# Attention and a gated block on one core: idle products on PE in the first stage, a shorter distance table, the remainder of v on halves of PE's columns, and a planner with other costs

## The chip, the cores and the metric

The program runs on one core of one Trainium2 chip. The metric is the time of one execution on the device in microseconds (us); the time of the kernel before is the median of three runs. Engines are named as the profile names them: PE does the matrix products, DVE is the vector engine, ACT the scalar engine, POOL the general one, and SP's queue issues the transfers.

## The reference

Eight batches, eight heads, 576 positions, 64 numbers a head. Attention looks back over a window of 128 positions with a slope a head (the distance table is `-8*slope*distance`, with a huge number where the mask is zero). Its result is the input of a block with a gate: a product with w_in, halves u and v, a normalisation of v, a mixing of v along the positions, a product with w_out.

```python
scores = scale * np.matmul(q, k.transpose(0, 1, 3, 2))
scores = np.where(mask, scores + bias[None], -1000000000.0)   # 0 <= rel < 128
attn = softmax(scores)                    # sum + 1e-9
x = np.matmul(attn, v)                    # -> [8, 576, 512]
h = np.maximum(x @ w_in, 0.0)             # 512 -> 1024
u, v = h[..., :512], h[..., 512:]
v_n = (v - mean(v)) / np.sqrt(var(v) + 1e-06)
v_s = np.einsum('ts,bsd->btd', w_spatial, v_n) + b_spatial[None, :, None]
out = (u * v_s) @ w_out
```

## The kernel before

Heads are taken in pairs: a batch has four pairs (p), and a pair has five tiles (t) of query blocks, the first with one block of 64 rows, the others with two. Float32 accuracy comes from splitting a number into two 16-bit parts, so a product is made of three.

**The first stage** is batch 0 (and pair 0 of batch 1), done without such a split: `raw_tile` and `raw_rest` make the scores as float32 products (L581, L582), take bias, minimum and exponential (DVE L614, ACT L619), turn the result around on PE (L651, L653), copy it (L325) and multiply with the values (L671). Beside it the weights are prepared: w_in comes as 64-bit numbers in four chunks a half (transfer L364, tile `vn`), which `words` turns into float32 (ACT L341, DVE L345 to L357) and `magnitudes` into absolute values (ACT L373, tile `ab`); the mixing weights (transfers L441 to L449, tile `gw`) get absolute values in ACT L460, L464, L465. `column_scale` sums such absolute values over the partitions on PE, with `ones` as the stationary operand (L384). `largest` finds the scale of a batch's values (ACT L554, DVE L502 and L503, PE L505, DVE L507, then POOL L524, L525 and DVE L527).

**Later batches** make the probabilities in two 16-bit parts (L720, L754, L759), a transposing transfer turns them around (L765), and `attention` multiplies them with the values on two halves of PE's columns at a time (L798: 72 products, in 36 pairs that write to partitions 0 to 63 and 64 to 127). Each pair of heads leaves a tile `xt` with the high part of x, a piece of R = 64 columns, and the low part: `tail` copies the last 64 low columns behind the high ones (L532, recorded in the helper's line L325), so that `v_rem` can use high and low part of the last 64 positions as one stationary operand of 128 columns.

**The gated block** (`gated`) has units of 12 to 14 products that fill the PE: `v_unit` (L864, 128x512 each, 12 a unit, four units a batch), `v_rem` for the last 64 positions (L886, 8 products of 128x512: a stationary operand for each of the four chunks, times two parts of w_in; upper and lower half of the result are added afterwards), `u_unit` (L916), `sp_unit` (L937) and `o_unit` (L965).

**The order** on every engine is made when the program is built: `Plan` collects each piece of work with its engine, a weight in ns, a due time and what it reads and writes; `order` is a list scheduler that models the engines (and two levels of PE's clock), and `emit` runs it forward and backward 20 times and takes the best. An engine then executes its work strictly in that order. A row of 64-row products and a row of 128-row products use PE's array in different shapes (64*64, 128*64, 128*128 in the rows); the planner has the constant SWITCH for that.

## Time and profile before

| what | value |
|---|---|
| median of 3 runs | 577.02 us (574.56 to 577.95) |
| the profiled execution's own time | 573.75 us |
| its span, first to last instruction | 572.0 us |
| PE busy | 542.9 us, 95% of the span |
| DVE busy | 466.8 us, 82% |
| ACT busy | 418.0 us, 73% |
| POOL busy | 65.7 us, 11% |

The shares are means over stages with different limits. The profiled execution lies 0.81 us below the fastest of the three timed runs, and 1.75 us of its time lie outside the span.

### The profile page before, as it was taken

The page shows a single profiled execution, that of the slowest core. Times are in us where ns is not written, and L with a number is a line of the kernel's source. Part 1 is how long each engine was busy: PE and PEld are TensorE (multiplying, and loading weights), DVE is VectorE, ACT ScalarE, POOL GpSimd, SP SyncE. Part 2 cuts the span into 40 slices and gives each one's busy share as a digit, 9 for nine tenths or more (in the row PEclk, how much of TensorE's full clock was granted, in tenths as well). Part 3 has the DMA queues.
Part 4 walks back from the last instruction along what each step waited for, and adds up shares of the span by engine and source line. Part 5 has one row for each costly group of instructions (what it writes and reads, how often), then busy time and mean ns, then how long its engine had stood idle before and what let it go on. Part 6 is the DMA issues. An engine that isn't in the chain of part 4 may idle for free.

```text
span 572.0 us, 16995 instructions
## 1 busy us (share of the span) xinstructions
PE 542.9 (95%) x6472; PEld 386.2 (68%) x6475; DVE 466.8 (82%) x1794; ACT 418.0 (73%) x1389; POOL 65.7 (11%) x124
## 2 busy tenths in 40 slices
PE   3399998899999999999999999999999999999997
PEld 2155646677668866787578757887587758785775
DVE  4779999999998589987899689888998788764541
ACT  5979999999996298767877587679996657543202
POOL 2001122000124002010131001200202011000000
PEclk9999999999999999999999999999999999999999
DMA  8961321698998275794468787769677650460002
GB/s 276 324 260 48 117 93 43 151 185 175 241 212 161 58 182 104 143 227 132 114 139 218 164 157 120 161 162 223 140 127 127 136 115 1 84 138 32 1 11 72
DMA packets 149845, 79.74 MB, mean 139 GB/s; under 512 B 129666, under 2 KB 139906, under 8 KB 149764
## 3 DMA queue, kind: packets, MB, share of 16 engines
q1 hardware_dynamic: 149764, 78.67, 58.8%
q8 instruction: 50, 0.82, 0.6%
q14 instruction: 31, 0.25, 0.1%
HBM read 37.13 MB, written 9.44 MB: 81 GB/s over the span
## 4 chain that ended last, share of the span: by engine, by line
PE 72%; DVE 1%; ACT 1%; issue 0%; ACTq 0%
PE m L937 17%; PE m L965 15%; PE m L916 14%; PE m L864 11%; PE x L798 6%; PE s L582 6%; PE m L886 2%; ACT prob L720 0%; ACT pq L754 0%; DVE st L825 0%; DVE vt L838 0%; ACT vt L329 0%; DVE vn L875 0%; ACT o L972 0%; DVE vn L325 0%
## 5 line engine op out<-in xcount | busy, mean ns | idle before, releaser
L720 ACT ACTIVATE prob<-prob,stat 64x64 f32<-64x64 f32 (+1 forms) x270 | 113.4, 424 | 15.1 <-DVE stat L714 15.0
L937 PE MATMUL m<-wsp,vn 128*128 128x288 f16 x768 | 113.0, 286 | 0.1
L916 PE MATMUL m<-xt,win 128*128 128x288 f16 x768 | 100.6, 286 | 1.2 <-DVE win L404 0.6
L965 PE MATMUL m<-gs,wout 128*128 128x288 f16 x768 | 100.2, 286 | 0.0
L754 ACT ACTIVATE pq<-prob,stat 64x64 f16<-64x64 f32 x270 | 93.8, 423 | 3.5 <-ACT prob L720 1.0
L759 DVE SCALAR_TENSOR_TENSOR pq<-prob,stat,pq 64x64 f16<-64x64 f32 x270 | 90.4, 378 | 2.0 <-ACT pq L754 1.8
L916 PEld LDWEIGHTS <-win 128*128 128x128 f16 x768 | 73.8, 98 | 22.5 <-issue 3.0
L937 PEld LDWEIGHTS <-vn 128*128 128x128 f16 x768 | 73.9, 98 | 21.2 <-issue 2.7
L965 PEld LDWEIGHTS <-wout 128*128 128x128 f16 x768 | 73.7, 98 | 20.8 <-issue 2.2
L864 PE MATMUL m<-win,xt 128*128 128x512 f16 x384 | 86.4, 379 | 0.9 <-ACT pq L325 0.9
L714 DVE CUSTOM_DVE_ANT_0 prob<-s,tab 64x64 f32<-64x64 f32 (+1 forms) x270 | 73.3, 317 | 7.2 <-PE s L582 7.1
L582 PE MATMUL s<-qkraw 64*64 64x192 f32 (+2 forms) x1116 | 60.0, 325 | 7.5 <-DMA qkraw<-in_qk_dram 6.1
L864 PEld LDWEIGHTS <-xt 128*128 128x128 f16 x384 | 36.9, 98 | 44.4 <-issue 1.9
L834 POOL TENSOR_TENSOR st<-st,nhalf 128x1 f32<-128x1 f32 (+1 forms) x40 | 29.2, 732 | 302.2 <-DVE st L830 289.3
L972 ACT ACTIVATE o<-m,am 128x288 f32<-128x288 f32 x49 | 24.2, 497 | 46.1 <-PE m L965 36.1
L945 DVE TENSOR_TENSOR u<-m,u 128x288 f32<-128x288 f32 x64 | 28.8, 450 | 35.1 <-PE m L937 35.0
L582 PEld LDWEIGHTS s<-qkraw 64*64 64x64 f32 x1116 | 41.4, 137 | 22.0 <-issue 10.8
L720 ACT ACTIVATION_READ_ACCUMULATOR prob<-prob,stat 64x1 f32 (+1 forms) x270 | 51.6, 191 | 0.0
L329 ACT ACTIVATE u<-m 128x288 f32<-128x288 f32 x57 | 23.0, 403 | 38.2 <-PE m L916 37.9
L798 PEld LDWEIGHTS <-vh 128*64 128x64 f16 x1296 | 39.9, 112 | 7.6 <-issue 7.3
L798 PE MATMUL x<-pt,vh 128*64 128x64 f16 (+1 forms) x1296 | 43.1, 205 | 0.1
L798 PE MATMUL x<-pt,vl 128*64 128x64 f16 (+1 forms) x648 | 40.1, 204 | 0.0
(154 smaller groups left out, 786.3 us busy)
## 6 DMA issues: line engine op xcount, KB each, us to landing
qkraw<-in_qk_dram SPq DMA_DIRECT2D x28, 576.0 KB, 4.2
vb<-in_v_dram SPq DMA_DIRECT2D x32, 320.0 KB, 5.0
out_dram<-o SPq DMA_DIRECT2D x64, 144.0 KB, 2.0
vn<-in_w_in_dram SPq DMA_DIRECT2D x8, 512.0 KB, 7.1
pt<-in_w_out_dram SPq DMA_DIRECT2D x4, 512.0 KB, 5.8
gw<-in_w_spT_dram SPq DMA_DIRECT2D x4, 288.0 KB, 8.1
qkraw<-in_qk_dram SPq DMA_DIRECT2D x3, 320.0 KB, 5.6
pt<-pq SPq DMA_TRANSPOSE x54, 5.3
```

What stands on the lines that cost most here:

```text
L582: nc.tensor.matmul(sc[j]()[out, at:at + k1 - k0], raw()[rows, 0, i * D:(i + 1) * D], raw()[rows, 1, k0:k1], start=True, stop=True, skip_gr ...
L714: nc.vector.tensor_tensor_reduce(pt(), sc[t][j]()[:m, SOFF[t]:SOFF[t] + n], tabs[h]()[:m, W - n:], -0.125, 3e38, ALU.add, ALU.min, st()[:m ...
L720: nc.scalar.activation(pt(), pt(), AF.Exp, bias=st()[:m, NM, j, t:t + 1], scale=-1.0, accum_out=st()[:m, SM, j, t:t + 1])
L754: nc.scalar.activation(pq[j]()[:m, 0, qs], prob[2 * (p % 2) + j]()[:m, cs], AF.Copy, scale=st()[:m, RC, j, t:t + 1])
L759: nc.vector.scalar_tensor_tensor(pq[j]()[:m, 1, qs], prob[2 * (p % 2) + j]()[:m, cs], st()[:m, RC, j, t:t + 1], pq[j]()[:m, 0, qs], ALU.mu ...
L798: nc.tensor.matmul(xp()[j * D:(j + 1) * D, x0:x0 + n * D], l()[:, kt, j * D:(j + 1) * D], rhs, start=(i > 4, j) not in seen, stop=False, s ...
L834: nc.gpsimd.tensor_tensor(st()[:m, 11:12], st()[:m, 10:11], nhalf()[:m], ALU.pow)
L864: nc.tensor.matmul(pt(), xt[c]()[:, X0[a] + t * P:X0[a] + (t + 1) * P], win()[:, c, w, DH:DF], start=(n == 0), stop=(n == 3 * NC_ - 1))
L916: nc.tensor.matmul(pt()[:, :HS], win()[:, c, w, d * P:(d + 1) * P], xt[c]()[:, X0[a] + hf * HS:X0[a] + (hf + 1) * HS], start=(n == 0), sto ...
L937: nc.tensor.matmul(pt()[:, :HS], l, r, start=(n == 0), stop=(n == len(ops) - 1))
L945: nc.vector.tensor_tensor(u(), pt()[:, :HS], u(), ALU.mult)
L965: nc.tensor.matmul(pt()[:, :HS], wout()[:, d, w, e * P:(e + 1) * P], gs[d]()[:, a, :], start=(n == 0), stop=(n == 3 * ND - 1))
```

## The change

Four things change. (1) `warm` puts 120 products of 128x192, in 24 pieces of five, into the plan; they multiply `ones` with the distance tables into a bank of the PSUM tag `x` that nobody reads. In the plan 16 pieces wait for ACT's second sum over the values, 8 for the absolute values of w_in; these waits exist in the plan alone, the instructions themselves wait for nothing but `ones`, the tables and the bank. (2) The distance table is made for 64 rows on POOL and copied to the other 64 by DVE. (3) `tail` is gone, `xt` is 64 columns shorter, and `v_rem` makes 12 products of 64x512, in six pairs, one of each pair on either half of PE's columns: high part times both parts of w_in, low part times the high part of w_in (the product of the two low parts is no longer made). (4) The planner no longer adds SWITCH to every piece; each piece has a mode for its first and last product (F: whole array, S: 64*64, X: 128*64), and a change of mode costs TURN = 95 ns. Weights of some pieces are set anew, and transfers issued between 1200 and 8000 ns land 1300 ns later in the plan.

```diff
+    TURN, NEAR = 95, 0
...
                     if e == "SP":
...
-                        end = dma + self.LAG[e]
+                        end = dma + self.LAG[e] + 1300 * (1200 <= now < 8000)
                     else:
+                        if e == "PE":
+                            weight += self.TURN * (modes[n][head] != mode)
+                            mode = modes[n][rear]
...
-            for a in (0, D):
-                rel = relf()[a:a + D]
...
-        plan.add("POOL", 2450, 0, f, (), [(relf, 0)])
+            rel = relf()[:D]
...
+        plan.add("POOL", 1250, 0, f, (), [(relf, 0)])
+        plan.add("DVE", 250, 800, lambda: nc.vector.tensor_copy(relf()[D:], relf()[:D]), [(relf, 0)], [(relf, 1)])
...
-    def tail(xt, due):
-
-        copy(R, lambda: (xt()[:, S:S + R], xt()[:, 2 * S:2 * S + R]), due, xcols(xt, 1, (NQ - 1) * P, S), [(xt, 2)], fast=True)
...
-        plan.add("PE", SWITCH // 2 + scored_ns(t), due, lambda: scored(sc, t, 0, raw), seen_by(raw, t) + [(ones, 0), (masked, 0)], [(sc[j], t) for j in range(2)])
+        plan.add("PE", scored_ns(t), due, lambda: scored(sc, t, 0, raw), seen_by(raw, t) + [(ones, 0), (masked, 0)], [(sc[j], t) for j in range(2)], "SS")
...
-                n = 0
-                for c in range(NC_):
-                    for w in range(2):
-                        nc.tensor.matmul(pt(), xt[c]()[:, (NQ - 1) * P:S + R], win()[:, c, w, DH:DF],
-                                         start=(n == 0), stop=(n == 2 * NC_ - 1))
-                        n += 1
+                sides = [[(0, w, c) for c in range(NC_)] + [(1, 0, c) for c in range(w, NC_, 2)] for w in range(2)]
+                for n, pair in enumerate(zip(*sides)):
+                    for side, (a, w, c) in enumerate(pair):
+                        nc.tensor.matmul(pt()[side * R:(side + 1) * R], xt[c]()[:, X0[a] + (NQ - 1) * P:X0[a] + S], win()[:, c, w, DH:DF],
+                                         start=(n == 0), stop=(n == 3 * NC_ // 2 - 1), skip_group_check=True)
...
+    idle = plan.buf(ps, "x", 2, [P, 512], F32)
+
+    def warm(n, k, due, after):
+
+        def f():
+            for i in range(n):
+                nc.tensor.matmul(idle()[:, :W], ones(), tabs[(k + i) % H](), start=True, stop=True)
+        plan.add("PE", n * pe(W, gap=2.5), due, f, after + [(ones, 0)] + [(tabs[(k + i) % H], 0) for i in range(n)], [(idle, k)])
...
+    for k in range(16):
+        warm(5, k, -20000 + 500 * k, [(am0, ("sum", 1))])
...
+    for k in range(16, 24):
+        warm(5, k, -20000 + 500 * k, [(wv[k % 4][1], 0)])
```

Line numbers of the changed kernel are other ones: its L588 and L589 are L581 and L582 here, L1020 is the idle product, L516 is L505, L395 is L384, L868 is L864, L890 is L886, L548 is L541, L558 is L551, L375 is L364, L452 to L460 are L441 to L449.

The first place is PE early in the first stage, after the second tile's scores of pair 0. Before, the scores of pair 1 and pair 2 follow one another (`s` is the scores' bank, `masked` fills what lies outside the window), then L505:

```order
L582 MATMUL s_69<-qkraw 64x192
L581 LDWEIGHTS ones
L581 MATMUL s_66<-masked,ones 64x64
L582 MATMUL s_66<-qkraw 64x128
L581 LDWEIGHTS ones
L581 MATMUL s_67<-masked,ones 64x64
L582 MATMUL s_67<-qkraw 64x128
L582 MATMUL s_66<-qkraw 64x192
L582 MATMUL s_67<-qkraw 64x192
L505 LDWEIGHTS ones
L505 MATMUL m<-wide,ones 128x128
```

In the changed kernel the idle products stand behind pair 1:

```order
L589 MATMUL s_69<-qkraw 64x192
L1020 LDWEIGHTS ones
L1020 MATMUL x<-tab_76,ones 128x192
L1020 LDWEIGHTS ones
L1020 MATMUL x<-tab_77,ones 128x192
```

30 of them, then L516, then 60 more, which end ahead of pair 2:

```order
L516 LDWEIGHTS ones
L516 MATMUL m<-wide,ones 128x128
L1020 LDWEIGHTS ones
L1020 MATMUL x<-tab_82,ones 128x192
...
L1020 MATMUL x<-tab_76,ones 128x192
L588 LDWEIGHTS ones
L588 MATMUL s_66<-masked,ones 64x64
L589 MATMUL s_66<-qkraw 64x128
```

The second tile's scores of pairs 2 and 3 moved behind 90 idle products; the last 30 stand between pair 3 and the twelve products of the mixing weights (L395, before L384).

The second place is SP's queue from its start (`qkraw` and `pt` are queries and keys of the four pairs, `vb` the values, `vn` the chunks of w_in, `gw` the mixing weights). Before:

```order
L541 DMA qkraw<-in_qk_dram 128x2x256 x3
L551 DMA vb<-in_v_dram 128x640
L541 DMA pt<-in_qk_dram 128x2x256
L551 DMA vb<-in_v_dram 128x640 x3
L364 DMA vn_161<-in_w_in_dram 128x1024
L364 DMA vn_169<-in_w_in_dram 128x1024
L364 DMA vn_175<-in_w_in_dram 128x1024
L441 DMA gw<-in_w_spT_dram 128x576 x4
...
L364 DMA vn_301<-in_w_in_dram 128x1024
L541 DMA qkraw<-in_qk_dram 128x2x320
```

Now:

```order
L548 DMA qkraw<-in_qk_dram 128x2x256 x3
L548 DMA pt<-in_qk_dram 128x2x256
L558 DMA vb<-in_v_dram 128x640 x3
L375 DMA vn_154<-in_w_in_dram 128x1024
L558 DMA vb<-in_v_dram 128x640
L375 DMA vn_162<-in_w_in_dram 128x1024
L375 DMA vn_167<-in_w_in_dram 128x1024
L375 DMA vn_173<-in_w_in_dram 128x1024
L452 DMA gw<-in_w_spT_dram 128x576 x4
...
L548 DMA qkraw<-in_qk_dram 128x2x320 x3
```

The keys of pair 3 moved ahead of the first values, the fourth chunk of w_in ahead of the mixing weights, and the second pieces of queries and keys ahead of the values of batch 1.

The third place is the remainder of v in batch 1 on PE. Before it stands between two v units:

```order
L864 LDWEIGHTS xt
L864 MATMUL m<-win,xt 128x512
L886 LDWEIGHTS xt
L886 MATMUL m<-win,xt 128x512
L886 LDWEIGHTS xt
L886 MATMUL m<-win,xt 128x512
```

Now it stands between the scores of a pair and a v unit:

```order
L589 MATMUL s_68<-qkraw 64x192
L890 LDWEIGHTS xt
L890 MATMUL m<-win,xt 64x512
L890 LDWEIGHTS xt
L890 MATMUL m<-win,xt 64x512
...
L890 MATMUL m<-win,xt 64x512
L868 LDWEIGHTS xt
L868 MATMUL m<-win,xt 128x512
```

Eight products of whole width became twelve of half width. Over the part of the program from the first attention (L798) on, PE changes the shape of its array 101 times before and 101 times now: from F to S 24 and 23 times, S to F 23 and 16, X to F 27 and 30, F to X 25 and 22, S to X 1 and 8.

## Rows read from the trace of the kernel before

**Rows 1.** The page's totals: busy us of each engine (share of the span) and instructions.
```profile
span 572.0 us, 16995 instructions
PE 542.9 (95%) x6472; PEld 386.2 (68%) x6475; DVE 466.8 (82%) x1794; ACT 418.0 (73%) x1389; POOL 65.7 (11%) x124
```

**Rows 2.** Busy time of the engines by stretch: the stretch in us from the span's start and its length, busy us (instructions) of each engine, PE's granted clock as a share of full speed, the share of the transfer engines, GB/s.
```profile
0.00:10.00 10.00, 1.95 (x22) 1.45 (x26) 3.44 (x32) 3.94 (x14) 3.83 (x14) 1.00 0.75 233
10.00:25.00 15.00, 6.01 (x44) 2.52 (x38) 13.44 (x58) 15.00 (x46) 0.90 (x2) 1.00 1.02 332
25.00:28.40 3.40, 2.53 (x12) 0.77 (x11) 1.05 (x3) 2.91 (x6) 0.00 (x0) 1.00 1.02 348
28.40:43.00 14.60, 14.24 (x106) 8.24 (x107) 11.40 (x50) 11.20 (x36) 0.53 (x2) 1.00 0.66 260
43.00:60.00 17.00, 15.64 (x207) 9.86 (x206) 16.05 (x63) 15.91 (x55) 2.83 (x10) 1.00 0.26 83
60.00:110.00 50.00, 44.71 (x492) 28.14 (x491) 48.12 (x170) 49.18 (x160) 8.43 (x13) 1.00 0.29 84
110.00:150.00 40.00, 39.58 (x643) 30.79 (x638) 39.61 (x178) 38.60 (x144) 3.56 (x9) 1.00 0.96 189
150.00:520.00 370.00, 370.00 (x4620) 269.98 (x4619) 310.72 (x1193) 269.69 (x913) 42.82 (x69) 1.00 0.66 143
```

**Rows 3.** The chain of work that ended last, where it runs through batch 1 and later ones, in order of time: start, us, engine, tile and line, number of instructions.
```profile
149.48 2.75 PE m L864 x12
152.23 1.73 PE m L886 x8
153.96 2.59 PE m L864 x12
156.84 1.28 PE s L582 x29
158.12 5.29 PE m L864 x24
163.41 1.55 PE x L798 x72
164.95 7.46 PE m L916 x60
...
370.25 1.28 PE s L582 x29
371.52 1.55 PE x L798 x72
```

**Rows 4.** PE in order of time in the first stage: start, us from the first start to the last end of the merged instructions, line, tile, shape of the array, size of one, number, idle time before it and its releaser.
```profile
11.59 0.66 PE L582 MATMUL s<-qkraw 64*64 64x128 f32 x2
13.24 0.90 PE L582 MATMUL s<-qkraw 64*64 64x192 f32 x6
14.27 0.26 PE L505 MATMUL m<-wide,ones 128*128 128x128 bf16 x1
14.62 0.90 PE L582 MATMUL s<-pt 64*64 64x192 f32 x7
25.56 0.40 PE L384 MATMUL m<-r,ones 64*128 64x288 bf16 x1 [2.80 <-ACT r L464]
26.59 1.14 PE L384 MATMUL m<-wsp,ones 128*128 128x288 bf16 x4
28.36 1.56 PE L582 MATMUL s<-qkraw 64*64 64x192 f32 x16
...
38.50 2.14 PE L671 MATMUL x<-pq,vb 128*64 128x64 f32 x24
42.46 0.61 PE L384 MATMUL m<-ab,ones 128*128 128x512 bf16 x1
43.29 0.70 PE L384 MATMUL m<-ab,ones 128*128 128x512 bf16 x2 [0.22 <-issue]
50.66 1.52 PE L671 MATMUL x<-pq,vb 128*64 128x64 f32 x29
```

**Rows 5.** ACT and DVE in order of time in the first stage, columns as in rows 4.
```profile
13.93 0.29 DVE L503 TENSOR_SCALAR wide<-ident,am 128x128 bf16<-128x128 f32 x1
25.53 0.68 ACT L465 ACTIVATE r<-gw 1x576 bf16<-1x576 f32 x1
27.28 0.43 DVE L345 TENSOR_SCALAR wx<-wx 128x512 f32<-128x512 f32 x1 [2.82 <-ACT wx L341]
29.65 0.63 ACT L373 ACTIVATE ab<-wx 128x512 bf16<-128x512 f32 x1 [1.69 <-DVE wx L357]
```

**Rows 6.** Early rows of DVE and ACT around the distance tables (L319), columns as in rows 4.
```profile
3.20 0.52 DVE L319 TENSOR_SCALAR tab<-u 128x192 bf16<-128x192 f32 x2 [1.72 <-POOL u L289]
4.52 0.22 DVE L614 CUSTOM_DVE_ANT_0 prob<-s,tab 64x64 f32<-64x64 f32 x1 [0.80 <-PE s L582]
8.55 0.74 ACT L554 ACTIVATE junk<-vb 128x640 f16<-128x640 f32 x1 [1.93 <-DMA vb<-in_v_dram]
```

**Rows 7.** PE in one attention, in pairs of half-width products (128x128 and 128x64), columns as in rows 4.
```profile
163.71 0.28 PE L798 MATMUL x<-pt,vh 128*64 128x128 f16 x4
163.83 0.22 PE L798 MATMUL x<-pt,vl 128*64 128x128 f16 x2
163.88 0.23 PE L798 MATMUL x<-pt,vh 128*64 128x64 f16 x4
```

**Rows 8.** The copies that `tail` makes, from the list of line L325: engine, number, min/median/max ns of one, first and last start in us.
```profile
L325 ACT COPY xt<-xt x22: 228/242/253, 79.2 to 505.4; 128x64 f16<-128x64 f16 x22
L325 DVE COPY xt<-xt x10: 130/178/182, 145.9 to 515.2; 128x64 f16<-128x64 f16 x10
```

60 lines of the change are left out of this document (33 added, 27 removed).

## The prediction

> **What bounds the kernel now.** I read the totals first: PE is busy for 95% of the span, DVE for 82%, ACT for 73% [rows 1]. The stretches then show that these means hide three regimes [rows 2]. From 150 to 520 us PE is busy for 370.00 of 370.00 us, while DVE (310.72) and ACT (269.69) have room: only PE's work counts there, and the chain of work runs through PE's units alone from 149.48 us on [rows 3]. From 43 to 150 us ACT is busy for 15.91 of 17, 49.18 of 50 and 38.60 of 40 us, and DVE for 16.05, 48.12 and 39.61: the two together are the limit, and PE still has 7.1 us idle (1.36, 5.29 and 0.42). Before 43 us the limits change: ACT is full from 10 to 25 us while the transfers run at 332 GB/s; from 25 to 43 us ACT is idle for 3.89 us (0.49 and 3.40) and DVE for 5.55 (2.35 and 3.20), and PE is busy for 14.24 of the 14.60 us from 28.4 on.
>
> That last stretch is where PE is slow. The granted clock reads 1.00 in every stretch [rows 2], but the rows show two levels: four products of 288 columns take 1.14 us with a last one of 0.40, that is 0.247 us apiece or 1.2 columns per ns, and one product of 512 columns takes 0.61 us at 42.46; from 43.29 on two of them take 0.70 us, and 29 products of 128x64 take 1.52 us where 24 took 2.14 at 38.50 [rows 4]. So PE ran at its 1.2 GHz level until about 43 us and at 2.4 GHz after it.
>
> **The remainder of v.** It costs 1.73 us for 8 products, 0.216 each [rows 3]. The new form makes 12 half-width ones in six pairs. If the two of a pair run at once, that is 6 x 0.216 = 1.30 us, 0.43 less. That they do is seen in the attention, the same array shape: three pairs of 128 columns start at 163.71 and the next group at 163.88, 0.057 us a pair, where 128 columns at 2.4 per ns last 0.053 [rows 7]. Seven of the eight lie where PE is the limit, so 7 x 0.43 = **3.0 us**. The first, in batch 0, lies where ACT and DVE are; I count nothing.
>
> The new shape could cost changes of shape. Rows price them: from a v unit to the scores the chain jumps from 153.96 + 2.59 = 156.55 to 156.84, 0.29 us; back from the scores, 24 products take 5.29 instead of 24 x 0.216 = 5.18, so 0.11; from the v unit to the attention 158.12 + 5.29 = 163.41 leaves nothing, and from the scores to the attention 370.25 + 1.28 = 371.53 neither [rows 3]. In the built order the changes of shape are 101 on both sides, F to S one fewer, S to F seven fewer, X to F three more; with 0.11 for X to F as for S to F that is -0.29 - 0.77 + 0.33 = -0.7 us. The difference is small and rests on single rows, so I take 0 (bounds -0.7 and, at 0.29 + 0.11 for every new v_rem, +2.8). The Trainium skill, TensorEngine Tiling (Array Packing), Key Properties, says that changing the tiling mode, not just the tile, drains the engine; by it every new v_rem would pay at both ends, as in the second rival, which the rows into X do not show.
>
> **The copies of tail.** They go: 22 on ACT of 0.242 us and 10 on DVE of 0.178 [rows 8]. Behind 150 us PE's work covers them (DVE is free for 59, ACT for 100 of the 370 us [rows 2]); without that cover they would cost what they take. Some 8 (two batches) can lie in the stretch that ACT and DVE bound, first at 79.2: 8 x 0.2 over two engines is 0.8 us at most; I take half, **0.4 us** (0 to 0.8).
>
> **Distance table and early transfers.** POOL stops sooner and the first table (3.20) is made earlier, but the first scores are only there at 4.52, and ACT waits for the values until 8.55 anyway [rows 6]. The copy costs DVE some 0.25 us of the 6.56 it has free in the first 10 us. Keys of pair 3 before values shift exponentials into ACT's wait and the first value sum back by one transfer: 0, bounds -0.6 and +1.0 us of gain. The 1300 ns act in the plan only.
>
> **The idle products.** They have no wait, so PE starts them when pair 1's scores end, 11.59 + 0.66 = 12.25 us [rows 4]. At the low level one takes 192 / 1.2 = 0.160 us, at the high one 0.0825 (192 / 2.4 and the 0.0025 by which 0.216 exceeds 512 / 2.4). When the level rises no row says: bounds are at the first product and never. The longest run of whole-array products that left it low is the 12 of 288 columns from 26.59 on (mixed with four before); the first 30 take 4.8 us, longer than those. I take the rise at their end, 17.05 us. L505's operand was ready at 13.93 + 0.29 in the old order; even 2 us later it hides. Then 60 x 0.0825 = 4.95, to 22.1; the scores of pairs 2 and 3, 0.90 + 0.90 at the low level [rows 4], take 0.9, to 23.0; 30 more, to 25.5; four products of L384, to 26.0. ACT's absolute values that L384 waits for next ended at 25.53 + 0.68 = 26.21 [rows 5]. Nothing is left over: the products just fit in, and behind them are queued pairs 2 and 3, for which DVE and ACT wait. Against that loss I set 0.5 us.
>
> The gain has two parts. The last eight products of L384, from 26.59 to 28.36, need half: 0.9 us. From 28.4 to 43 us PE's 14.24 us of work shrink to 7.1, so that ACT (11.20) and DVE (11.40) become the limit; at the same kind of work and the high level, from 43 to 60 us, they were still idle for 6% [rows 2]. So the stretch lasts 11.4 / 0.94 = 12.1 us instead of 14.6: 2.5 us. That the level holds through such work is seen after 43 us, where 50.66 is still fast. The fourth chunk of w_in, behind which DVE waited 2.82 us at 27.28 and ACT 1.69 at 29.65 [rows 5], now lands before the mixing weights; its idle time lies partly in the same stretches, and ACT pays with 1.1 us of such work ahead of L465; I add 0.5. Together -0.5 + 0.9 + 2.5 + 0.5 = **3.4 us**. Bounds: nothing, if ACT and DVE are full anyway, and 4.7, the mean of their idle time from 25 to 43 us. What follows until 150 us is bound by ACT and DVE, so an earlier start there comes through to the end.
>
> **Sum.** 3.0 + 0.4 + 3.4 = 6.8 us. Against the profiled execution that is 573.75 - 6.8 = 566.95. That execution lies below all three timed runs; against their median, 577.02 - 6.8 = **570.2 us**. About 0.5%, 2.9 us, is what a measurement of this kernel can tell from no change.
>
> **Rivals.**
> - *Only the remainder pays.* The level rises, but the first stage is held by transfers (1.02 of the engines until 28.4 us [rows 2]) and by ACT's full queue. For it: ACT had no idle time from 10 to 25 us. Against: 3.4 us of idle on ACT behind 28.4, where the transfers thin out to 0.66. 577.02 - 3.0 - 0.4 = 573.6.
> - *Each new remainder pays for its shape*, 0.29 + 0.11 at both ends, and keeps 0.03 of 0.43: 577.02 - 0.2 - 0.4 - 3.4 = 573.0. Against: the rows into X without a gap.
> - *The halves take turns*: 12 x 0.216 = 2.59, 0.86 more than now, 7 x 0.86 = 6.0: 577.02 + 6.0 - 3.8 = 579.2. Against: 0.057 us a pair.
> - *Slower: the level stays low.* For it: from 28.36 to 42.46 PE worked almost without a gap and it did not rise. Then PE needs 12.25 + 4.8 + 9.6 + 1.8 + 4.8 = 33.25, and 12 products of 0.24 more, to 36.1, where the old order reached 28.36: 7.8 us later, the 3.4 lost, 577.02 - 3.4 + 7.8 = 581.4. Each product at the low level costs 0.0775 more; it decides from the point at which about 44 of the 90 later ones run low (3.4 us) and the level does not hold behind 28 us either. The Trainium skill, TensorE: Matmul & The Clock Gate, Part 1, says that the throttled state is the default and activity releases it; by that the level would rise, as at 43 us. Its Part 4 says that transposes do not count as busy in the same way, which would fit the long low stretch.
> - *The new order.* All weights changed, so every engine's order did; a stall of a few us in the stretch to 150 us could eat the gain: about 577.
>
> **Chances and range.** Forecast 0.56; only the remainder 0.17; paying for its shape 0.07; halves in turns 0.05; low level 0.09; new order 0.06. Faster by over 0.5% means below 574.1: the forecast, the shape case, and half of "only the remainder" (its 573.6 lies close to the bound): 0.71. Slower: 0.05 + 0.09 = 0.14. Same: the rest, 0.15. The forecast's own range goes by the bounds: at best 3.0 + 0.7 + 0.8 + 4.7 + 1.0 = 10.2 us, 566.8, at worst 3.0 + 0.5, 573.5. The range is 565.8 to 577.5: the best case with 1 us for the spread of a median of such runs (574.56 to 577.95), up to no change, without the two slower cases (0.14).
>
> **What would show it.** Right: products of L1020 0.08 us apart from about 17 us on; the first scores of the third tile (L589 with 16 products) near 27.5 us and 0.8 us long instead of 1.56; L890 in six steps of 0.216; PE's idle time from 150 us on still nil; 60 to 110 us with ACT at 98%. Wrong: idle products 0.16 us apart beyond the first 30, L395 waiting for PE rather than for ACT, L890 taking 2.6 us, or a PE gap over 2 us between 43 and 150 us.

## The result, and the profile after

The change made the kernel slower by about 1%: 580.99 us, the median of seven executions (578.57 to 585.37), against 574.89 us for the kernel before in the same job (seven, 573.46 to 577.95); the ratio is 1.0105 with a 95% interval of 1.0061 to 1.015. The forecast was 570.2 us, 565.8 to 577.5. The profiled execution of the changed kernel took 581.23 us, its span is 579.5 us, 7.5 us more than that of before. One execution, of the ten of e12 below, took 920.48 us at a mean granted clock of 0.668; it has no part in any comparison.

The page's totals of the changed kernel, busy us (share of the span) and instructions, to be held against [rows 1]:

```profile
span 579.5 us, 17296 instructions
PE 553.7 (96%) x6627; PEld 398.1 (69%) x6627; DVE 466.3 (80%) x1781; ACT 419.5 (72%) x1371; POOL 59.4 (10%) x121
```

PE is busier, DVE and ACT as busy as before: the totals tell little. PE's work in the first stage tells more, in order of time (columns as in [rows 4], rows left out where the dots stand; L1020 is the idle product, L589 the scores, L395 the sums over the absolute values):

```profile
10.40 4.46 PE L1020 MATMUL x<-tab,ones 128*128 128x192 bf16 x30
...
15.73 5.11 PE L1020 MATMUL x<-tab,ones 128*128 128x192 bf16 x60
20.77 0.22 PE L588 MATMUL s<-masked,ones 64*64 64x64 bf16 x2
...
25.81 0.28 PE L395 MATMUL m<-r,ones 64*128 64x288 bf16 x1 [1.08 <-ACT r L475]
26.51 0.28 PE L395 MATMUL m<-r,ones 1*128 1x288 bf16 x1 [0.42 <-ACT r L476]
...
27.32 0.52 PE L395 MATMUL m<-r,ones 64*128 64x288 bf16 x2
27.77 1.55 PE L589 MATMUL s<-qkraw 64*64 64x192 f32 x16
...
39.90 1.80 PE L395 MATMUL m<-ab,ones 128*128 128x512 bf16 x4
```

Sixty idle products take the 5.04 us from 15.73 to 20.77, 0.084 us apiece: the high level, as forecast. At 27.77 the sixteen scores of the third tile take 1.55 us, as in [rows 4]: the low level is back, and at 39.90 it still is. Cut at the places where the granted clock changes, and at 150 us, the stretches of the changed kernel read so (columns as in [rows 2]; the clock's column is the one after the five engines; ahead of 14.2 us the profile has no record of the clock, and the 1.00 there is none either: the first 24 idle products start 0.16 us apart, which is the low level):

```profile
0.00:14.20 14.20, 7.65 (x61) 6.06 (x61) 8.12 (x56) 9.06 (x33) 2.84 (x11) 1.00 0.81 271
14.20:27.80 13.60, 11.28 (x135) 9.48 (x133) 11.24 (x37) 12.40 (x29) 1.41 (x2) 1.00 1.04 358
27.80:41.50 13.70, 13.54 (x101) 7.67 (x100) 9.61 (x44) 9.54 (x30) 0.53 (x2) 0.50 0.68 260
41.50:48.30 6.80, 4.88 (x69) 3.03 (x70) 6.37 (x27) 5.53 (x17) 1.44 (x5) 1.00 0.01 2
48.30:55.10 6.80, 6.80 (x52) 3.91 (x51) 6.17 (x23) 6.06 (x24) 0.00 (x0) 0.50 0.08 20
55.10:89.30 34.20, 30.74 (x349) 17.79 (x347) 31.22 (x110) 33.23 (x103) 5.38 (x11) 1.00 0.32 104
89.30:96.10 6.80, 5.65 (x34) 3.04 (x29) 6.04 (x19) 5.46 (x14) 1.72 (x2) 0.50 0.28 87
96.10:150.00 53.90, 53.53 (x745) 41.36 (x744) 51.14 (x217) 50.48 (x178) 9.11 (x20) 1.00 0.71 156
150.00:579.50 429.50, 419.64 (x5105) 305.76 (x5103) 336.35 (x1254) 287.71 (x951) 36.98 (x70) 1.00 0.59 127
```

Three things are to be seen: the level falls three times after it has risen; PE has 9.86 us idle from 150 us on (429.50 - 419.64), where before it had 3.8, all of it behind 520 us; and from 96.1 us on the level stays. I take a span as PE's work at the high level, plus PE's idle time, plus half of what PE was busy at the low level. Before, 25.0 us of PE's work lay ahead of 43.5 us, at the low level: 12.5 us lost, 29.1 us idle, work 530.4. Now 33.6 us lay at the low level (the rows at 0.50 and 7.65 us ahead of 14.2): 16.8 lost, 25.8 idle, work 536.9. By cause:

| where | us |
|---|---|
| idle products: 9.9 us of work, 9.2 less idle and 1.9 less at the low level ahead of 43 us | -1.2 |
| what is left of PE's work | -3.4 |
| low level behind 43 us (half of 6.80 + 5.65) | +6.2 |
| idle behind 150 us | +6.1 |
| idle from 43 to 150 us | -0.2 |
| sum | +7.5 |

Two of these rows are less firm than they look. Half is too much for the low level: 32 products that take 2.57 us at it take 1.59 at the high one (e2 and e9 below), 38% less, and by that share the falls behind 43 us cost an estimated 4.7 us and not 6.2. And the row of -3.4 is only what the sum leaves over, so it holds that error too; the remainder of v can be 1.5 of it (e16 and e17 below), and in the middle of the program, where most of the remainders lie, PE is busy for 1.0 us longer than before, not shorter (370.15 and 369.11 us in the rows further down).

The gaps behind 150 us, PE's rows with their releasers, and then ACT's at the third of them:

```profile
275.08 1.63 PE L968 MATMUL m<-gs,wout 128*128 128x288 f16 x12 [1.20 <-ACT o L975]
...
404.05 1.63 PE L968 MATMUL m<-gs,wout 128*128 128x288 f16 x12 [2.07 <-ACT o L975]
```

```profile
402.23 1.38 ACT L759 ACTIVATE pq<-prob,stat 64x64 f16<-64x64 f32 x4 [0.97 <-DMA pt<-pq]
403.52 0.48 ACT L975 ACTIVATE o<-m,am 128x288 f32<-128x288 f32 x1
```

PE's o unit (L968) needs a bank of tag `m`, which ACT frees when it copies an earlier o out (L975); that copy stands in ACT's order behind four instructions that make pq, and at 402.23 those had waited 0.97 us for a transposing transfer. In three batches the same place waits (339.09 too, 1.12 us).

A measure that is used below: the time from the remainder of v of the second batch to that of the last, between which PE does the same work in all orders with the same remainder. Before, after, and the fastest kernel below (e9), by stretch:

```profile
152.07:521.18 369.11, 369.11 (x4616) 269.58 (x4614) 308.65 (x1179) 267.62 (x905) 42.82 (x69) 1.00 0.65 142
```
```profile
152.57:528.34 375.77, 370.15 (x4715) 270.41 (x4711) 311.30 (x1193) 273.63 (x916) 34.20 (x65) 1.00 0.65 141
```
```profile
150.88:518.55 367.67, 367.67 (x4639) 268.34 (x4638) 307.25 (x1170) 264.30 (x887) 42.33 (x69) 1.00 0.66 142
```

The changed kernel comes to the first mark 0.5 us later than before, needs 6.66 us more between the two, and 0.3 us more behind: in its profiled execution most of the loss lies where I had taken PE's zero idle time for granted. Of the 6.66 us, 5.62 are PE's idle time. A fall of the level between the marks counts into this measure too; the changed kernel's profile has none there.

### The profile page after: what moved, and what is told of

Read it like the earlier page. It is cut to its first block, busy times and chain, and to the rows that moved or that the text cites. A ratio compares the mean times of both kernels' runs of the same rounds, so it can differ in the third digit from the quotient of the medians.

```text
span 579.5 us, 17296 instructions
## 1 busy us (share of the span) xinstructions
PE 553.7 (96%) x6627; PEld 398.1 (69%) x6627; DVE 466.3 (80%) x1781; ACT 419.5 (72%) x1371; POOL 59.4 (10%) x121
## 4 chain that ended last, share of the span: by engine, by line
PE 59%; ACT 13%; DVE 12%; DMA 11%; issue 2%; POOL 1%; SPq 1%; ACTq 0%; DVEq 0%; POOLq 0%
PE m L940 18%; PE m L919 13%; PE m L968 10%; PE s L589 5%; DMA pt<-pq 5%; PE m L868 4%; PE x L803 4%; ACT prob L725 3%; DMA out_dram<-o 2%; ACT pq L759 2%; DVE st L829 2%; DVE pq L764 2%; PE x L678 2%; DMA gw<-in_w_spT_dram 1%; POOL st L838 1%
## 5 line engine op out<-in xcount | busy, mean ns | idle before, releaser
L968 PE MATMUL m<-gs,wout 128*128 128x288 f16 x768 | 101.1, 286 | 4.8 <-ACT o L975 4.8
L919 PE MATMUL m<-xt,win 128*128 128x288 f16 x768 | 102.2, 289 | 1.8 <-ACT u L340 0.9
L759 ACT ACTIVATE pq<-prob,stat 64x64 f16<-64x64 f32 (+1 forms) x270 | 95.6, 423 | 7.7 <-DMA pt<-pq 2.4
L764 DVE SCALAR_TENSOR_TENSOR pq<-prob,stat,pq 64x64 f16<-64x64 f32 (+1 forms) x270 | 92.1, 378 | 3.2 <-ACT pq L759 2.7
L919 PEld LDWEIGHTS <-win 128*128 128x128 f16 x768 | 75.4, 99 | 24.6 <-issue 4.6
L968 PEld LDWEIGHTS <-wout 128*128 128x128 f16 x768 | 73.6, 98 | 26.8 <-issue 8.5
L868 PE MATMUL m<-win,xt 128*128 128x512 f16 x384 | 87.4, 382 | 0.1
L340 ACT ACTIVATE u<-m 128x288 f32<-128x288 f32 x61 | 24.6, 406 | 69.4 <-PE m L919 69.2
L868 PEld LDWEIGHTS <-xt 128*128 128x128 f16 x384 | 36.7, 98 | 45.9 <-issue 5.5
L589 PE MATMUL s<-qkraw 64*64 64x192 f32 (+2 forms) x1116 | 58.7, 324 | 6.2 <-DMA qkraw<-in_qk_dram 4.3
L589 PEld LDWEIGHTS s<-qkraw 64*64 64x64 f32 x1116 | 41.7, 137 | 16.4 <-issue 7.0
L975 ACT ACTIVATE o<-m,am 128x288 f32<-128x288 f32 x46 | 22.6, 495 | 29.3 <-PE m L968 20.7
```

The source lines that it names most:

```text
L589: nc.tensor.matmul(sc[j]()[out, at:at + k1 - k0], raw()[rows, 0, i * D:(i + 1) * D], raw()[rows, 1, k0:k1], start=True, stop=True, skip_gr ...
L759: nc.scalar.activation(pq[j]()[:m, 0, qs], prob[2 * (p % 2) + j]()[:m, cs], AF.Copy, scale=st()[:m, RC, j, t:t + 1])
L764: nc.vector.scalar_tensor_tensor(pq[j]()[:m, 1, qs], prob[2 * (p % 2) + j]()[:m, cs], st()[:m, RC, j, t:t + 1], pq[j]()[:m, 0, qs], ALU.mu ...
L868: nc.tensor.matmul(pt(), xt[c]()[:, X0[a] + t * P:X0[a] + (t + 1) * P], win()[:, c, w, DH:DF], start=(n == 0), stop=(n == 3 * NC_ - 1))
L919: nc.tensor.matmul(pt()[:, :HS], win()[:, c, w, d * P:(d + 1) * P], xt[c]()[:, X0[a] + hf * HS:X0[a] + (hf + 1) * HS], start=(n == 0), sto ...
L968: nc.tensor.matmul(pt()[:, :HS], wout()[:, d, w, e * P:(e + 1) * P], gs[d]()[:, a, :], start=(n == 0), stop=(n == 3 * ND - 1))
```

## The experiments

Theory A: the idle products raise the level early, and the work behind them lets it fall again. Theory B: the planner's new costs make an order in which PE waits. Theory C, formed after the first four runs: any order made anew is slower than that of before. "Middle" is the measure above, "idle" PE's idle time from 150 us to the end, both of the profiled execution. Where an order is "kept", only what a piece of work issues was changed, not what the planner sees of it.

| kernel | order | median us | ratio to before, 95% | middle | idle |
|---|---|---|---|---|---|
| before | | 574.89 | | 369.1 | 3.8 |
| changed | new | 580.99 | 1.0105 (1.0061 to 1.015) | 375.8 | 9.9 |
| e1 | of changed | 585.16 | 1.0176 (1.0127 to 1.0224) | 380.0 | 14.3 |
| e2 | of before | 574.69 | 0.9991 (0.9967 to 1.0016) | 367.7 | 4.6 |
| e3 | of before | 576.46 | 1.0012 (0.9983 to 1.004) | 369.7 | 4.1 |
| e4 | new | 579.92 | 1.0091 (1.0063 to 1.012) | 379.5 | 13.9 |
| e5 | new | 579.83 | 1.008 (1.004 to 1.0121) | 370.7 | 7.9 |
| e6 | new | 581.95 | 1.0117 (1.0055 to 1.0179) | 382.7 | 13.4 |
| e7 | new | 579.78 | 1.008 (1.0051 to 1.0108) | 372.3 | 6.8 |
| e8 | new | 579.06 | 1.0062 (1.0033 to 1.009) | 371.8 | 5.7 |
| e9 | of before | 573.08 | 0.9964 (0.9941 to 0.9988) | 367.7 | 3.7 |
| e10 | of changed, o moved | 591.80 | 1.0306 (1.0276 to 1.0336) | 390.2 | 20.5 |
| e11 | new | 577.40 | 1.0035 (1.0007 to 1.0063) | 370.9 | 5.8 |
| e12 | new | 575.34 | 0.9996 (0.9971 to 1.0021) | 369.7 | 4.1 |
| e13 | of changed | 576.84 | 1.0022 (0.9994 to 1.005) | 379.0 | 11.4 |
| e14 | of changed, o moved | 580.84 | 1.0124 (1.0055 to 1.0193) | 379.3 | 12.0 |
| e15 | of before | 574.29 | 0.9984 (0.9959 to 1.0009) | 367.7 | 3.7 |
| e16 | of before | 574.66 | 0.9983 (0.9962 to 1.0004) | 369.1 | 3.8 |
| e17 | of before | 573.12 | 0.9959 (0.9937 to 0.998) | 369.2 | 4.9 |

**e1, the changed kernel without its idle products.** They stay in the plan, so the order is kept.

```diff
-            for i in range(n):
-                nc.tensor.matmul(idle()[:, :W], ones(), tabs[(k + i) % H](), start=True, stop=True)
+            pass
```


> The changed kernel with its order untouched on every engine; only the 120 idle products are not issued. Theory A (the idle products raise PE's level at 14 us, but the work of the first stage lets it fall at 27.8, and again at 48.3 and 89.3 us, so that PE is low for longer than without them): the level rises once, near 43 us, and stays; the time is about 3 us shorter than the changed kernel's, 578 us. Theory B (the idle products are without effect, the new order on all engines costs the time): 580 to 582 us, with PE's gaps of 1 to 2 us near 275, 339 and 404 us as they were. My prediction's reasons would want it slower than the changed kernel by 3 us, 584.

585.16 us, 4 us slower than with them, and near the 584 that my prediction's reasons asked for. The idle products are not what costs. But the reasons are not borne out: in the profiles both kernels come to the remainder of the second batch at the same time (152.53 us without, 152.57 with), and what differs is PE's idle time behind 150 us, 14.3 and 9.9 us, in the same order. The falls at 48.3 and 89.3 us are there without the idle products, and so are the waits for o.

**e2, the remainder of v alone**, order of before kept: six pairs in place of eight products, the copies of tail not issued.

```diff
...
-                        nc.tensor.matmul(pt(), xt[c]()[:, (NQ - 1) * P:S + R], win()[:, c, w, DH:DF], ...
+                        nc.tensor.matmul(pt()[side * R:(side + 1) * R], xt[c]()[:, X0[a] + (NQ - 1) * P:X0[a] + S], ...
```


> The kernel before with its order untouched; only the remainder of v is made in six pairs of half-width products, and the copies of tail are planned but not issued. If the pairs run at once and the change of shape costs little, as predicted: 7 x 0.43 = 3.0 us less than before, 572, or 571.5 with the copies. If each remainder pays 0.4 us for its shape: 575, as before.

No gain in the median. In the rows (PE in order of time) there is one, but a small one:

```profile
152.07 2.75 PE L864 MATMUL m<-win,xt 128*128 128x512 f16 x12
154.75 1.49 PE L886 MATMUL m<-win,xt 128*64 128x512 f16 x12
156.17 2.76 PE L864 MATMUL m<-win,xt 128*128 128x512 f16 x12
158.86 0.50 PE L582 MATMUL s<-qkraw 64*64 64x64 f32 x6
```

From start to start the v unit takes 2.68 us, the remainder 1.42, the next v unit 2.69: 6.79 for the three. Before, the first v unit started at 149.48 and took 2.59 (to the next start), and the scores behind the same three started 7.00 us later, at 156.48. So a remainder in pairs saves 0.21 us, not 0.43: it pays 0.09 us on the way into the half-width shape and 0.12 on the way out. That the median did not show these 1.5 us has to do with the level, which fell in two stretches of the profile:

```profile
67.50:74.30 6.80, 6.41 (x54) 4.39 (x55) 5.28 (x14) 5.24 (x17) 0.00 (x0) 0.50 0.01 2
...
91.40:94.80 3.40, 3.40 (x21) 1.77 (x19) 3.37 (x11) 2.68 (x8) 0.00 (x0) 0.50 0.25 66
```

The profile of before had no such falls, but other executions of before read a lower mean clock: of 23 in this job, the six at 1.00 took 572.92 to 573.72 us, the other seventeen (0.991 to 0.997) 573.9 to 577.8. I had read the stages from an execution of the better kind. Of e2's ten executions only one reads 1.00 (572.25 us); its other nine (0.990 to 0.994) have a mean of 574.64 us, against 575.86 for the seventeen of before. So at a like clock e2 is 1.0 to 1.2 us faster, which agrees with the rows.

**e3, idle products alone**, order of before kept: 88 of them in PE's waits from 15.5 to 26.6 us.

```diff
+                    if h == 0 and step == HS:
+                        idle((8, 8, 8, 30, 4, 0)[c])
...
-        ... lambda: scored(sc, t, 0, raw), ...
+        ... lambda: (scored(sc, t, 0, raw), idle(30 if (b, p, t) == (0, 3, 1) else 0)), ...
```


> The kernel before with its order untouched; 88 idle products stand only where its PE waited: 30 behind the scores of pair 3 (15.5 us), 8 behind each of the first three products of the mixing weights, 30 behind the fourth, 4 more before the last: PE is dense until the scores at 28.4 us. Theory A: the level rises near 19 us, but falls during the float32 work behind 28.4 us even without a gap ahead of it; no gain, 573 to 577 us. If it was the gap ahead of the scores that let it fall in the changed kernel: the level holds and the stretch from 28.4 to 43 us gets 2 to 3 us shorter, 571 to 572 us. Theory B expects no effect, 575.

576.46 us: nothing gained. The level was high from 18.0 us on, fell at 31.6 and again at 65.8 and 89.6: theory A. But PE was not dense, as the run had meant it to be. The scores of the third tile ran at the high level, then PE waited 1.65 us, and the level fell in the transposes and products with the values behind that wait:

```profile
26.98 0.88 PE L584 MATMUL s<-qkraw 64*64 64x192 f32 x16
29.51 1.05 PE L663 MATMUL m<-ident,prob 64*64 64x64 f32 x6 [1.65 <-DVE wam L389]
```

So this run does not tell the kind of work from the waits.

**e4, the changed kernel without idle products in the plan either**, so ordered anew.

```diff
-    for k in range(16):
-        warm(5, k, -20000 + 500 * k, [(am0, ("sum", 1))])
...
-    for k in range(16, 24):
-        warm(5, k, -20000 + 500 * k, [(wv[k % 4][1], 0)])
```


> The changed kernel without idle products in the plan as well, so that its planner, with the new costs, makes another order. Theory A: without them the level rises once, and the remainder gains 3.0 us: 572 us, if the new planner's order is as dense as the old one's. Theory B (the new costs make worse orders): PE has gaps of several us behind 150 us and the time is 577 to 582 us.

579.92 us, although the level rose at 36.9 us and did not fall again before 272 us. The remainder of the second batch came at 146.98 us, 5.1 us earlier than before, and the middle took 10.3 us more, 1.7 of them in a fall from 272.4 to 275.8 us, just behind a wait of PE for o (2.11 us). That fits theory B, though the run does not part the new costs from the new work; and the early arrival is worth nothing here.

**e5 to e8: which part makes the order.** e5 is the changed kernel with the planner's costs of before, e6 the changed kernel with the later landing undone, e7 the work of before with the new costs, e8 the work of before with the new remainder and the old costs.

```diff
e5, e6
-                        end = dma + self.LAG[e] + 1300 * (1200 <= now < 8000)
+                        end = dma + self.LAG[e]
e5 also, at each of seven pieces
-        plan.add("PE", sum(scored_ns(t) ...
+        plan.add("PE", SWITCH + sum(scored_ns(t) ...
```


> The changed kernel's work (idle products, short table, remainder of v in pairs, no copies of tail) ordered by the planner with the costs of before: SWITCH on its pieces, no modes, no later landing. Theory B, the new costs made the slow order: about 573 us (570 to 576), and PE without a gap of over 1 us between 150 and 520 us. Theory C, any order made anew lands some us above the one of before, whatever the costs: 578 to 583 us, with gaps of 1 to 2 us on PE behind ACT's copies of o or behind another late operand. Theory A, the idle products cost the time: 580 us.

> The changed kernel with one of its two new costs undone: transfers issued between 1200 and 8000 ns land as early in the plan as before; the modes stay. If the later landing made the slow order: 573 us (570 to 576). If the modes and new weights made it: 579 to 582 us, with PE waiting 1 to 2 us for ACT's copies of o between 270 and 410 us again. Theory C: 578 to 583 us.

> The work of before, all of it, ordered by the planner with the new costs (modes, new weights, later landing). Theory B: as slow as the changed kernel less what its work saves, 578 to 583 us, with PE gaps of over 1 us behind 150 us. If the new costs are harmless and the new work brings the slow order: 573 to 576 us. Theory C: 578 to 583 us.

> The kernel before with the remainder of v in six pairs and without the copies of tail, ordered anew with the costs of before. By my sum 3.4 us faster than before: 571 us. Theory B: 571 to 575 us. Theory C: 578 to 583 us. If the six pairs bring nothing, as with the order of before kept, and the order is as good: 574 to 575 us. The step itself: L885 in six pairs of 0.216 us, 1.30 us a batch.

All four lie 0.6 to 1.2% above before, which speaks for theory C and against a single guilty cost. But the middles part them: 371 to 372 us with either the old costs or the old work, 376 to 383 with new costs on new work (changed, e4, e6; in e4 and e6 an estimated 1.7 and 3.3 us of it are falls of the level at PE's waits, the rest is PE's idle time but for about 1 us). e5 and e8 lose elsewhere: e5's profiled execution comes to the second remainder at 158.41 us, after falls of the level from 66.2 to 76.4 and from 90.1 to 96.9 us; e8 took 573.4 and 575.3 us in two executions with a mean clock of 0.993 and 0.994, and 578.7 to 580.9 in eight with 0.985 to 0.988.

**e11 and e12: one number of the planner moved**, the work of before.

```diff
e11
-    SWITCH = 190
+    SWITCH = 200
e12
-    LAG = {"PE": 260, "DVE": 150, "ACT": 170, "POOL": 200, "SP": 1600}
+    LAG = {"PE": 260, "DVE": 150, "ACT": 180, "POOL": 200, "SP": 1600}
```


> The kernel before, all its work and its planner, with one number of the planner moved: SWITCH 200 in place of 190 ns. Theory C, an order made anew lands where it lands, and the one of before is a good draw: 576 to 582 us. If only large changes of the costs or of the work bring slow orders: 574 to 575 us.

> The kernel before, all its work and its planner, with another number of the planner moved: what ACT's results take to be seen, 180 in place of 170 ns. Theory C: 576 to 582 us, and not the time of the kernel with SWITCH 200. If only large changes bring slow orders: 574 to 575 us.

577.40 and 575.34 us, against 575.07 for before in this job: ten nanoseconds in a constant are worth up to 0.35%, but not 1%. Theory C holds only in this weaker form: two orders made anew by such a small change cost 2.3 and 0.3 us, and those made for larger changes 4.5 to 7.4.

**e9, the level held.** e2 with 22 more idle products: 6 near 64 us, 8 near 67 us, 8 near 90 us.

```diff
+                if (b, p, t, j) == (1, 0, 3, 0):
+                    for i in range(8):
+                        nc.tensor.matmul(tp()[:, :W], ones(), tabs[i % H](), start=True, stop=True)
...
+            for i in range({(0, 2, 3): 6, (0, 0, 4): 8}.get((b, p, t), 0)):
+                nc.tensor.matmul(tp()[:, :W], ones(), tabs[i % H](), start=True, stop=True)
```


> The order of before, untouched, with the remainder of v in six pairs, the copies of tail not issued, and 22 idle products of 128x192 added on PE at three places where the level fell soon after in the run of the remainder alone: 6 near 64 us and 8 near 67 us, in front of products with the values, and 8 near 90 us, in front of transposes that wait for ACT. If PE's granted clock falls between 60 and 95 us because of the work there, and idle products can hold it: no stretch at the low level behind 44 us, clock 1.0 from 43 us on, and 572 to 573 us in nearly all executions (the one execution of the remainder alone that the records show at 1.00 throughout took 572.25). If idle products can't hold it there: the falls stay and the time is 575 to 576.5 us. The idle products themselves cost 22 x 0.0825 = 1.8 us, of which 1.3 lie in waits that are there anyway.

573.08 us, faster than before by 0.36% (0.12 to 0.59%). The mean clock reads 0.999 or 1.000 in all ten executions, and in all 24 of e16 and e17 below; of before's 25 in this job five read 1.000 and twenty 0.991 to 0.997. The same place on PE, first in e2, then in e9 and last in the profile of before:

```profile
66.03 0.83 PE L671 MATMUL x<-pq,vb 128*64 128x64 f32 x16 [0.43 <-DVE xt L680]
67.58 2.57 PE L671 MATMUL x<-pq,vb 128*64 128x64 f32 x32 [0.72 <-ACT xt L325]
```
```profile
66.06 0.83 PE L676 MATMUL x<-pq,vb 128*64 128x64 f32 x16
66.82 0.83 PE L669 MATMUL m<-tab,ones 128*128 128x192 bf16 x8
67.59 1.59 PE L676 MATMUL x<-pq,vb 128*64 128x64 f32 x32
```
```profile
66.36 0.83 PE L671 MATMUL x<-pq,vb 128*64 128x64 f32 x16 [0.42 <-DVE xt L680]
67.91 1.59 PE L671 MATMUL x<-pq,vb 128*64 128x64 f32 x32 [0.72 <-ACT xt L325]
```

Eight idle products fill the wait of 0.72 us, and the 32 products behind it take 1.59 us where they took 2.57 in e2. One pair of profiles would not show what did it: the profile of before has the same waits as e2 and 1.59 us all the same, because the level did not fall in that execution. It is the clock of the 34 executions that shows it. The idle products both fill the waits and put whole products of 16 bits among float32 work; no run does the one without the other.

**e13, the same in the changed kernel**, its order kept: 50 idle products near 44, 46, 86 and 90 us.

```diff
+            for i in range({(0, 0, 2): 6, (1, 0, 3): 12}.get((b, p, t), 0)):
+                nc.tensor.matmul(tp()[:, :W], ones(), tabs[i % H](), start=True, stop=True)
...
+            idle({(1, 0, 2): 24}.get((b, p, t), 0))
```


> The changed kernel in its own order with 50 more idle products on PE: 14 near 44 and 46 us, 24 near 86 us (in a wait of 2.73 us) and 12 near 90 us (in a wait of 1.15 us), ahead of the places where its level fell. If the falls cost what the accounting says: no stretch at the low level behind about 42 us, PE's loss to it there 6.2 us less or nearly so, its waits grow by up to half of that, and the time falls from 581 to 575 to 578 us. If PE's order behind 150 us alone makes the kernel slow: 580 to 582 us with the level held.

576.84 us, 4.1 less than the changed kernel, and 2.0 above before, which is not clear of zero (0.9994 to 1.005). In the profile there is no fall from 40.9 us to 402.7, and the remainder of the second batch comes at 149.04 us, 3.5 earlier than in the changed kernel's. So the falls behind 43 us are shown to cost some 4 us of the 6.2 that the accounting gives them. The idle time of 11.4 us and the middle of 379.0 (with a fall at 402.7, behind a wait for o of 1.99 us) are those of the slowest of the ten executions, 580.23 us; they do not tell what the other nine, 574.12 to 579.91 us, waited for.

**e10 and e14: copies of o earlier on ACT**, the changed kernel. e10 moves every one in front of up to four ACT instructions, e14 only the three at these gaps.

```diff
-        for n, k, _ in best[1]:
-            self.ops[n][0][k][2]()
+        seq = [(n, k) for n, k, _ in best[1]]
+        for n in self.early:
...
+            while passed < 4 and seq[to - 1][0] not in waits:
+                to -= 1
+                m, w = seq[to]
+                passed += self.ops[m][0][w][0] == "ACT"
+            seq.insert(to, seq.pop(i))
```


> The changed kernel in its own order, except that every copy of o on ACT stands up to four ACT instructions earlier. If PE waits for o at 275, 339 and 404 us because ACT has four instructions that make pq in front of the copy: these gaps (1.2, 1.1 and 2.1 us) go, PE's idle time behind 150 us falls from 9.9 us to about 5, and the time from 581 to 576 or 577 us. If ACT is late there by its whole load, the gaps stay or move to another operand: 580 to 583 us.

> The changed kernel in its own order, with three copies of o on ACT (in batches 4 to 6 of eight, counted from 1) in front of the four instructions that make pq, and nothing else moved. If these four, 1.38 us, are what PE waits for: the gaps at 275, 339 and 404 us shrink from 1.2, 1.1 and 2.1 us to 0.7 or less, and the time falls by 2.5 to 4 us, to 577 to 578.5 us. If what the copy waits for is late itself, or the pq behind it then comes late for the next attention: the gaps stay or move, 580 to 582 us.

In both the gain that I hoped for failed to come; e14's other case (580 to 582 us) came. e10 took 591.8 us, outside both of its cases. In e14 the gap near 404 us went, the one near 272 us shrank to 0.34, one of 1.60 stayed near 338, and new ones came up (1.24 at 168.76 for a transposed pq, some of 0.3 to 0.4 for o and vt): idle 12.0 us, no gain. The order of these four instructions alone is not the cause. I take ACT to be late there with all its work. What ACT waits for from 150 to 530 us (us in total, times, longest) shows how the two orders differ, before first:

```profile
ACT u L329 <- PE m L916: 24.7, 16, 4.5
ACT o L972 <- PE m L965: 21.4, 16, 2.7
```
```profile
ACT u L340 <- PE m L919: 54.8, 19, 4.5
...
ACT o L975 <- PE m L968: 8.5, 13, 1.2
```

Before, ACT's free time is spread over the u and the o units. In the changed kernel it lies in the u units, and ACT has hardly any left in the o units, where its copies free PE's banks. By stretches of a batch, changed kernel:

```profile
300.00:310.00 10.00, 10.00 (x84) 7.98 (x83) 5.18 (x15) 1.01 (x3) 2.22 (x7) 1.00 0.60 173
...
330.00:340.00 10.00, 8.88 (x157) 7.09 (x156) 9.22 (x43) 9.91 (x39) 0.00 (x0) 1.00 1.14 225
340.00:345.00 5.00, 5.00 (x94) 3.17 (x94) 4.03 (x22) 5.00 (x23) 0.00 (x0) 1.00 1.02 205
```

ACT (fourth of the engines) has 1.01 us to do in ten of the u units, and is full for 14.91 of 15 us at the batch's end. Over nine kernels ACT's wait for u and the middle go together in the main: 20.2 to 24.7 us of wait with 367.7 to 371.8 (before, e5, e8, e9, e11), 35.3 with 372.3 (e7), 52.3 to 56.4 with 375.8 to 382.7 (changed, e4, e6). That is a correlation: no run moved this alone. The same rows hold a rival. The share of the transfer engines (last but one) is 1.14 and 1.02 at the batch's end, where no ten microseconds of before from 250 to 370 us read more than 0.95, and ACT's own wait at 402.23 us was for a transposing transfer. Whether ACT's work or the transfers are bunched first was not tested.

e14 showed something else by chance. In its profiled execution the level held from 13.3 to 44.0 us, and the first stage went as I had forecast it:

```profile
28.48 0.88 PE L601 MATMUL s<-qkraw 64*64 64x192 f32 x16
```
```profile
28.40:43.00 14.60, 12.58 (x159) 7.70 (x158) 14.27 (x68) 13.54 (x44) 1.96 (x7) 1.00 0.66 258
```

ACT and DVE are full, the first v unit starts at 49.14 us (53.49 in the changed kernel's profile, 52.51 before), and the second batch's remainder comes at 148.32, 4.25 us earlier than in the changed kernel's profile. Its span is 579.2 us, only 0.3 less. What took the rest back is not parted: the three moved copies differ too, and e1 has shown that the waits behind 150 us vary by 4 us in one order.

**e15, e9 with the 88 early idle products of e3.**

```diff
 (e9)
+                    if h == 0 and step == HS:
+                        idle((8, 8, 8, 30, 4, 0)[c])
```


> The kernel of the held level (order of before, remainder of v in pairs, 22 idle products near 64, 67 and 90 us: 573.1 us) with the 88 early idle products of the run with idle products alone. If raising the level early is worth something once it is held later: the scores of the third tile at the high level, and 570 to 572 us. If the first stage gives it back, as the falls at 28 and 32 us in the other runs say: 573 to 575 us, with a stretch at the low level between 28 and 45 us.

574.29 us: the early products bring nothing here either; the level was low from 30.1 to 43.8 us.

**e16 and e17: the remainder's worth with the level held in both.** e16 is e9 with the old remainder and tail, e17 is e9 again.

```diff
e16 (to e9)
...
-                        nc.tensor.matmul(pt()[side * R:(side + 1) * R], xt[c]()[:, X0[a] + (NQ - 1) * P:X0[a] + S], ...
+                        nc.tensor.matmul(pt(), xt[c]()[:, (NQ - 1) * P:S + R], win()[:, c, w, DH:DF], ...
```

> The kernel before in its own order, remainder of v of eight whole products and copies of tail as they were, with the 22 idle products near 64, 67 and 90 us. By the step between units in the traces (from 7.00 to 6.79 us for two v units with the remainder between them) the pairs save 0.21 us in each of seven batches, so this kernel takes 1.5 us more than the one with the pairs beside it. By my sum it takes 3.4 us more. If the pairs bring nothing: the same. If the level is held here too, it is faster than before by what the falls cost, 1 to 2 us: 573 to 574 us, clock 1.0 from 44 us on.

> The kernel of the held level once more, unchanged (order of before, remainder of v in pairs, no copies of tail, 22 idle products): 572 to 573.5 us, faster than before by 0.2 to 0.6%, and 1.5 us below the kernel beside it if the step between units tells what the pairs save.

574.66 and 573.12 us, 1.54 us between the medians (between the means 1.4, give or take 1.2); each still spreads over 4 us (570.7 to 575.29 in e17) with the level held, so the middles tell it better: 369.11 in e16 and 367.67 in e9, 0.24 us in each of six batches, 1.7 for seven. (e17's own middle holds one batch that took 1.5 us longer, with a wait of 1.06 us at 341.95.) The other half of e16's expectation, 573 to 574 us, was missed: with the old remainder the held level brings 0.4 us in the median (0.9962 to 1.0004 of before), less than the 1 to 2 us I had put on the falls.

Part of the spread is the first stage, and it is worth a look, because e9 and e17 are one program. In e9's profile the high level begins at 37.8 us, in e17's at 43.5; the mean clock does not count this, as the records begin there. The same row in both, e9 first:

```profile
38.22 1.36 PE L676 MATMUL x<-pq,vb 128*64 128x64 f32 x24
```
```profile
37.89 2.14 PE L676 MATMUL x<-pq,vb 128*64 128x64 f32 x24
```

The first v unit starts at 50.14 and 52.19 us, the second batch's remainder at 150.88 and 152.91, and the spans are 569.0 and 572.5 us: 2 us from the moment of the rise, 1.5 from the one batch. So in this pair of profiles, in the order of before, an earlier rise is kept to the end.

## Why the prediction was wrong, point by point

- **The remainder, 3.0 us: mis-sized.** The halves do run at once, but each remainder pays 0.09 + 0.12 us for its shape: 1.5 us measured. The step that failed is "I take 0" for the changes of shape, and it rested on two rows of the chain [rows 3] that I misread. The 0.29 us from the v unit to the scores hold five products of the scores. And the 0.11 us that I gave to the way back from the scores are paid at the other end, on the way into the attention, of which I said that it "leaves nothing". The starts of PE's rows in the kernel before show both:

```profile
153.79 2.75 PE L864 MATMUL m<-win,xt 128*128 128x512 f16 x12
156.48 0.50 PE L582 MATMUL s<-qkraw 64*64 64x64 f32 x6
```
```profile
162.59 0.81 PE L864 MATMUL m<-win,xt 128*128 128x512 f16 x3
163.34 0.30 PE L798 MATMUL x<-pt,vh 128*64 128x128 f16 x4
```

  Twelve products last 2.69 us up to the scores, where 12 x 0.216 are 2.59; three last 0.75 up to the attention, where 3 x 0.216 are 0.65. So the way into half-width products cost 0.10 us in the kernel before already, as in e2. The Trainium skill, TensorEngine Tiling (Array Packing), Key Properties, has the engine drained at a change of the tiling mode; the rows of e2 agree with it at both ends, with these numbers. The copies of tail (0.4) cannot be told apart in e16 against e17.
- **The idle products: the level rose, earlier than I took it (by 14.2, not at 17.05 us), and did not hold.** The step that failed is "that the level holds through such work is seen after 43 us". One profile showed it; the next execution need not. The level fell in float32 scores, transposes and products with the values, in the changed kernel at 27.8, 48.3 and 89.3 us, and in e2 and e3 too. I first took the work alone for the reason, but PE had waited shortly ahead of each of these falls: 1.08 and 0.42 us ahead of 27.8, 0.98 ahead of 48.3, 2.73 ahead of 89.3, 0.43 and 0.72 ahead of 67.5 (e2), 1.65 ahead of 31.6 (e3). Waits alone do not decide it either: e14 had 1.09 and 0.42 us in the same place as the changed kernel and held the level to 44.0 us. The Trainium skill, TensorE: Matmul & The Clock Gate, Part 4, says that PE's transposes do not count as busy like products; such rows stand ahead of the falls near 67 and 90 us, and whole products of 16 bits put between them held the level (e9), while no run takes transposes alone.
- **What the first stage gains comes through to the end: not seen in the new orders.** I wrote that what follows until 150 us is bound by ACT and DVE, "so an earlier start there comes through to the end". Up to 150 us that was right: in e14, whose order there is the changed kernel's, the held level brought the first v unit 4.35 us and the second batch 4.25 us forward. (Against before the first v unit is 3.4 us early. That this is the size of my term is in part luck, as the two orders differ.) Behind 150 us, of which I had said that only PE's work counts, 0.3 us of the 4.25 were left in the profile, and nothing of e4's 5.1. In the order of before the gain was kept (2 us, e9 against e17), and by the medians so were the 3.5 us by which e13 came earlier to the second batch.
- **The new order: the rival had 0.06 and the wrong place.** I looked for a stall ahead of 150 us and took PE's 370.00 of 370.00 us behind it as a property of the work. It was one of the order. With new costs on new work the middle takes 6.7 to 13.6 us more than before, falls of the level included. I had the instructions' order of PE's engine and of SP in view, but for ACT only busy shares over hundreds of microseconds, in which an ACT that is full for 15 us of a batch and idle for 9 looks the same as one with even load.
- **The base.** The forecast started from 577.02 us, the median of three; over all jobs before took 574.5 to 575.1. With the lower base the forecast would have been 2 us lower still, so this hid 2 us of the miss.

Settled by runs: the falls behind 43 us cost some 4 us (e13); the remainder in pairs, in the order of before, is not what made the kernel slower (e2, e9), nor are the idle products (e1); and the order keeps PE waiting behind 150 us (all profiles in the order of before have 3.7 to 4.9 us idle there, all in that of the changed kernel 9.9 or more). Not settled: what in the new costs places ACT's work so, whether the transfers do it, and how much of the wait the faster executions of e13 have.

## What to carry to other kernels

Where a scheduler makes the order, price a change with the order kept and again with the order made anew: here the remainder was worth 1.5 us in the old order and the held level 0.4 (e16 against before) to 1.6 (e9 against e2, from two jobs), while every larger change planned anew lost 4.5 to 7.4 us. Before you take a full engine as given, look stretch by stretch at the engine that frees its buffers, and at the transfers. And here idle products paid in the waits just ahead of the places where the level fell, not early on (e3, e15). To price a change of shape, take the starts of PE's rows: a chain of merged pieces can hide work in the step.
